# Residuals and a second bias preloaded into PSUM ahead of the products, in a transformer block kernel

## The chip, the cores and the metric

The kernel runs on one core of one Trainium2 chip. The metric is device time in microseconds of one execution. Three executions of the kernel before gave 504.6 us (median), 504.41 us and 506.51 us. The engines of the core are TensorE (PE in the profile; its weight loads are PEld), VectorE (DVE), ScalarE (ACT), GpSimd (POOL) and SyncE (SP, which here only issues DMAs). PSUM is the on-chip memory that the matmuls write into; it has eight banks of 128 x 512 fp32.

## What is computed

A pre-norm transformer block on x of 2048 tokens by 512 features, in fp32: sliding-window attention (32 heads of 16, window of 8 with dilation 2), its output product with a residual, and a second part with a squared ReLU. Cut to what matters here:

```python
h  = x + attention(layernorm(x)) @ wo            # the residual x is added to the output product
r  = relu(layernorm(h) @ w1 + b1)                # 512 -> 1792
h2 = h + (r * r) @ w2 + b2                       # 1792 -> 512, the second bias b2
```

## The kernel before

The 2048 tokens are 16 tiles of 128 rows, numbered `t`, in four groups `u = t // 4` of four tiles. Every fp32 product is made of three matmuls of operands split into a high and a low part (`mm3`, line 218): high x high, low x high, high x low. A product of 512 x 512 for one tile is 12 matmuls of 128 x 128 by 128 x 512.

The program is written out by hand in slots: a slot issues the PE work of a stretch, and then the chores that are due on the other engines. `at(d, f)` puts a chore among those at the end of the slot that is `d` ahead, `after(d, f)` behind these, and between the two `pump` issues pieces of attention on DVE until the DVE work that has been planned (`now["dve"]`) is as long as the PE work (`now["pe"]`). Every chore on DVE adds its planned time with `dve(...)`, so a chore that leaves DVE lets attention be issued earlier. Each engine carries out its own instructions in the order in which they were issued.

Attention is on DVE, POOL and ACT: DVE multiplies the queries with the keys (L340) and sums (L374), takes the maximum (L391) and subtracts it (`ex<-ex,mx`, L393); ACT takes the exponential (L397); DVE multiplies with the values (L351), POOL adds up (L408) into the output tile `o`. The queries come to PSUM with a copy by ACT (`qp`, L268).

The work has three stretches:

- up to about 165 us, the query, key and value products of all tiles (in four PSUM banks by turns), and between them the output products of tiles 0 to 3;
- from there to about 420 us, for u = 0, 1 and 2, the 14 slots of the second part of group u. A slot has `mlp1` (12 matmuls, L228, into a bank of two that take turns, `mm1` and `mm0`), whose ReLU with bias is taken by ACT (`hidden`, L876, then the square L877 and the high part `rh`, L152), and, three slots later, `mlp2` (12 matmuls, L900, that sum into four banks `acc` over all slots). In the same slots attention goes on for the next group, and the output products of its four tiles (`wo_product`, line 688) are put between, into the same two banks as `mlp1`;
- the last group, u = 3, with products put together in another way (L823).

What belongs to one output product of tile `t`, before the change: ACT puts the attention output `o` into two planes (`turn_split`, L621), a DMA transposes them, ACT joins them (`turn_join`, L630) and takes the high part `oh` (or `ohl` for every fourth tile, t = 2, 6, 10, 14; the name of its pool differs only), DVE the low part `ol`. Then PE runs 12 matmuls `wo`. Then `h_add` (line 664): DVE adds the residual out of SBUF to the PSUM bank (`h<-wo,h`, L666), and `norm_stats` takes mean and variance of the sum on DVE (L163, L164) and has POOL make the scale of them (three small instructions, `rs`). Then ACT normalises (`hn<-h,rs`, L196), POOL adds the second bias b2 to h (`add_b2`, L679), and h is written to DRAM (`spill`) to be read back when group t // 4 is finished. At the end of a group, `finish` (line 904) adds h to each `acc` on DVE (L908) and writes out.

SBUF tiles of 128 x 512 come from one ring of 15 (`row`).

Of the kernel before, what the change touches and what calls it, by code (L numbers as in the profile page):

```python
# [17 lines left out]
KB = D // P  # L18
FB = F // P
R = 4  # L20
# [38 lines left out]
def block_kernel(ctx, tc, x, wqkv, wo, w1, b1, w2, b2, out):  # L59
# [113 lines left out]
                                    scalar2=-1.0, op0=ALU.mult, op1=ALU.mult)  # L173
        (at if soon else after)(0, finish)

    def act_stats(key, src):

        nm = small.tile([P, 2], F32, name="nm", bufs=3)
        sq = small.tile([P, 1], F32, name="sq", bufs=3)
        rs = small.tile([P, 2], F32, name="rs", bufs=4)  # L180
        scrap = row("scrap")
        nc.scalar.activation(scrap, src, AF.Identity, accum_out=nm[:, 0:1])
        nc.scalar.activation(nm[:, 1:2], nm[:, 0:1], AF.Identity, scale=-1.0 / D)
        nc.scalar.activation(scrap, src, AF.Square, bias=nm[:, 1:2], accum_out=sq)
        stats[key] = nm, rs

        def finish():
            nc.gpsimd.tensor_scalar(out=rs[:, 1:2], in0=sq, scalar1=1.0 / D, scalar2=EPS,
                                    op0=ALU.mult, op1=ALU.add)
            nc.gpsimd.tensor_tensor(out=rs[:, 0:1], in0=rs[:, 1:2], in1=mhalf, op=ALU.pow)  # L190
            nc.gpsimd.tensor_tensor(out=rs[:, 1:2], in0=nm[:, 1:2], in1=rs[:, 0:1], op=ALU.mult)
        after(0, finish)
# [22 lines left out]
            lo(nc.vector, d, src, h)  # L215
            dve(0.16 + 0.53 / len(h_dst))

    def mm3(ps, lh, ll, rh, rl, mid=None, at_=2 * KB, lows_last=False):


        terms = [[(l, r, k) for k in range(KB)] for l, r in ((lh, rh), (ll, rh), (lh, rl))]
        if lows_last:
            terms[1:] = terms[:0:-1]
        terms = sum(terms, [])
        for n, (l, r, k) in enumerate(terms):
            if mid and n == at_:
                mid()
            nc.tensor.matmul(ps, l(k), r(k), start=(n == 0), stop=(n == 3 * KB - 1))  # L228


    items = [(s, g0, 2) for g0 in range(0, G, 2) for s in range(RI)]
# [39 lines left out]
    def attention():  # L271
# [40 lines left out]
        for n in range(N + 1):  # L312

            new, old = n < N, n > 0
            while new and not ready(n):
                yield None
            ng = ng1 = 0
            if new:
                s, g0, ng = items[n]
                u, b, e, i0 = where(s)  # L320
                HG = ng * GH
                for j in range(2):
                    load_k(n, j)
                if (n, 0) not in qps:
                    next_q(n, 0)
                lf = logits[:, n % 2, :RI * W * HG].rearrange("p (i w h) -> p i w h", i=RI, w=W)
                mx = small.tile([P, RI, HG], F32, name="mx")
            if old:
                s1, g1, ng1 = items[n - 1]
                e1 = ex.pop(n - 1)  # L330
                sm = small.tile([P, RI, ng1 * GH], F32, name="sm")
                if s1 not in o_t:
                    o_t[s1] = att.tile([P, RI, D], F32, name="o", bufs=3)

            def dots(j):
                kwin = window(ks[n, j], s, [1, GC])
                pr = att.tile([P, RI, W, GH, DH], F32, name="pr", bufs=3)
                if j % 2 == 0:
                    qps["now"] = qps.pop((n, j))
                nc.vector.tensor_tensor(  # L340
                    out=pr.rearrange("p i w h d -> p i w (h d)"),
                    in0=qps["now"][:, j % 2].unsqueeze(2).to_broadcast([P, RI, W, GC]),
                    in1=kwin, op=ALU.mult)
                load_k(*ahead(n, j, 2))
                return pr

            def weigh(j):
                load_v(n - 1, j)
                vwin = window(vs[n - 1, j], s1, [DH, GH], [1, DH])
                p2 = att.tile([P, RI, W, GH, DH], F32, name="pr", bufs=3)  # L350
                nc.vector.tensor_tensor(  # L351
                    out=p2, in1=vwin, op=ALU.mult,
                    in0=e1[:, :, :, j * GH:(j + 1) * GH].unsqueeze(4).to_broadcast(
                        [P, RI, W, GH, DH]))
                sums.append((p2, o_t[s1], (g1 + j) * GC, s1))
                load_v(*ahead(n - 1, j, 2))

            for j in range(max(ng, ng1)):
                if j < ng:
                    pr = dots(j)  # L360
                    yield 1.22
                if old and j == 0:
                    nc.vector.tensor_reduce(out=sm, in_=e1.rearrange("p i w h -> p i h w"),
                                            axis=X, op=ALU.add)
                    yield 0.23 + 0.035 * ng1
                if 0 < j < ng1 or 0 < j == ng1 < ng:
                    if j == 1:
                        nc.vector.tensor_tensor(
                            out=e1, in0=e1, op=ALU.mult,
                            in1=sm.unsqueeze(2).to_broadcast([P, RI, W, ng1 * GH]))  # L370
                    weigh(j - 1)
                    yield 1.55 if j == 1 else 1.26
                if j < ng:
                    nc.vector.tensor_reduce(out=lf[:, :, :, j * GH:(j + 1) * GH], in_=pr, axis=X,  # L374
                                            op=ALU.add)
                    yield 1.22
                    if j % 2:
                        next_q(*((n, j + 1) if j + 1 < ng else (n + 1, 0)))
                if old and j == 0:
                    nc.vector.reciprocal(sm, sm)  # L380
                    yield 0.26
            if new and b == 0:
                nc.vector.tensor_tensor(
                    out=lf, in0=lf, op=ALU.add,
                    in1=mask[:, i0:i0 + RI].unsqueeze(3).to_broadcast([P, RI, W, HG]))
                yield 0.16 + 0.07 * ng
            if old and ng1 >= ng:
                weigh(ng1 - 1)
                yield 1.26
            if new:  # L390
                nc.vector.tensor_reduce(out=mx, in_=lf.rearrange("p i w h -> p i h w"), axis=X,  # L391
                                        op=ALU.max)
                nc.vector.tensor_tensor(out=lf, in0=lf, op=ALU.subtract,  # L393
                                        in1=mx.unsqueeze(2).to_broadcast([P, RI, W, HG]))
                ex[n] = lf
                yield 0.42 + 0.15 * ng
                nc.scalar.activation(lf, lf, AF.Exp, scale=DH ** -0.5)  # L397
# [263 lines left out]
        hi_T(tr, hs_)  # L661
        lo_T(tr, hs_, ls_)

    def h_add(t, ps):
        h = hs[t]
        nc.vector.tensor_tensor(out=h, in0=ps, in1=h, op=ALU.add)  # L666
        dve(0.7)
        if t in AS:
            after(0, act_stats, t, h)
        else:  # L670
            norm_stats(t, h, R <= t < 14)

    def h_norm(t):
        hn[t] = row("hn")
# [9 lines left out]
    def unspill(t):  # L684
        hs[t] = row("h")
        nc.sync.dma_start(hs[t], h_d[t])

    def wo_product(t, slots):
        ps = turn["mm"].tile("wo")
        oh, ol = oT.pop(t)  # L690
        mm3(ps, lambda k: oh[:, k, :], lambda k: ol[:, k, :],
            lambda k: wo_h[:, k, :], lambda k: wo_l[:, k, :], lows_last=t in OV)
        for n, (fn, a) in zip(slots, ((h_add, (t, ps)), (h_norm, (t,)), (add_b2, (t,)),
                                      (spill, (t,)))):
            (at if fn is h_add else after)(n + (fn is add_b2), fn, *a)

# [190 lines left out]
    def mlp2(u, f, acc, js, first=False, last=False, mid=None):  # L889
# [7 lines left out]
        for n, (l, w, j) in enumerate(terms):  # L897
            if mid and n == len(terms) // 2:
                mid()
            nc.tensor.matmul(acc[j], l[:, j * P:(j + 1) * P], w[f],  # L900
                             start=(first and n < len(js)),
                             stop=(last and n >= len(terms) - len(js)))

    def finish(t, a):
        u, i = divmod(t, R)
# [106 lines left out]
    def first_phase(t0):  # L1012
        def chores(m):
# [15 lines left out]
                dve(HOLD)  # L1029
            for t in range(R):  # L1030
                if k == OT[t]:
                    at(0, load_h, t)
                    o_T(t)
                if t in HV and k == HK[t][0]:
                    at(0, h_split, t)
                    after(0, turn_dma, ("h", t))
                if t in HV and k == HK[t][1]:
                    at(0, turn_join, ("h", t))
                if k == WO[t]:
                    wo_product(t, (1, 3, 4, 6))  # L1040
                    now["pe"] += 2.73
# [53 lines left out]
    for u in range(R - 1):  # L1095
# [11 lines left out]
        for i in js:  # L1107
            t = R * (u + 1) + i
            if not end:
# [10 lines left out]
                if t in HV:  # L1120
                    h0 = 11 + i
                    turned += [(h0, midway, 0, h_split, t), (h0, after, 0, turn_dma, ("h", t)),
                               (h0 + 2, at, 0, turn_join, ("h", t))]
                for p, *what in ((LH[i] - a, at, 0, load_h, t), *turned,
                                 (WP[i] - a, wo_product, t, (0, 1, 2 + 3 * a + b, 3 + 3 * a + b))):
                    todo.setdefault(p, []).append(what)
                p, h = (HP[i], i % 2) if u < 2 else HL[i]
# [16 lines left out]
        for p in range(FB + LAG):  # L1144
            more = 0.0
            if p == FB:
                run(due)
                dve(HOLD)
            if u < 2 and p == FB - 2:
                dve(HOLD)  # L1150
            for fn, *a in sorted(todo.get(p, []), key=lambda x: x[0] is wo_product):
# [107 lines left out]
```

## Time and profile before

| | us |
|---|---|
| median of three executions | 504.6 |
| the profiled execution, first to last instruction (its span) | 501.7 |
| PE busy | 496.2, 2422 matmuls |
| DVE busy | 382.9 |
| ACT busy | 298.3 |
| POOL busy | 356.2 |
| DVE, adds of the residual (L666), 16 | 10.9 |
| DVE, statistics of h (L163), 16 | 11.1 |
| POOL, adds of b2 (L679), 16 | 21.2 |

An engine is busy from the start to the end of each of its instructions. Matmuls overlap in the pipeline, so the busy time of PE does not say that it ran at its peak: the distance from one matmul's start to the next's says more. A wait is put down to the instruction whose end let the waiting one go. The profiled execution ends 2.9 us before the median time of the three; what lies around the span (start and end of an execution) is in the time and not in the span.

### The profile page before, as it was taken

Reading aid. Unit: us, or ns where it says so; the run is one execution under the profiler, and the core shown is the slowest. Engines: PE = TensorE matmul, PEld = TensorE weight load, DVE = VectorE, ACT = ScalarE, POOL = GpSimd, SP = SyncE. Lnnn points to the kernel's source line nnn. Section 1 sums busy time; section 2 is a strip of 40 time slices with the busy share of each in tenths; the row PEclk is TensorE's granted clock in tenths of the full one; section 3 lists DMA queues with packets and bytes.
Section 4 is the critical chain, followed back from the end, with each engine's and each line's share of the span. In section 5 each row is a group of like instructions: output and inputs, shape, how many; then the busy total and the mean of one; then the engine's idle time right before and its main releaser. Section 6 shows DMA issues by size and latency. Waiting matters only on the chain.

```text
span 501.7 us, 7533 instructions
## 1 busy us (share of the span) xinstructions
PE 496.2 (99%) x2422; PEld 421.2 (84%) x2422; DVE 382.9 (76%) x520; ACT 298.3 (59%) x538; POOL 356.2 (71%) x434
## 2 busy tenths in 40 slices
PE   8999999999999999999999999999999999999997
PEld 7999888888888888888888888888888888998986
DVE  6479899988989989788879998888975147833223
ACT  4635777668346758378564555755555837666551
POOL 5714898886685999969777877769799464775610
PEclk9999999999999999999999999999999999999999
DMA  9668979989698989679577756967665472354112
GB/s 275 202 205 243 300 237 312 270 273 275 212 223 256 299 277 260 205 216 237 190 254 209 215 146 192 237 209 242 210 159 115 112 197 84 137 161 143 64 43 84
DMA packets 109359, 102.61 MB, mean 205 GB/s; under 512 B 29448, under 2 KB 77832, under 8 KB 109320
## 3 DMA queue, kind: packets, MB, share of 16 engines
q1 hardware_dynamic: 108376, 101.61, 69.5%
q10 hardware_dynamic: 944, 0.52, 0.3%
q8 instruction: 19, 0.31, 0.3%
q14 instruction: 20, 0.16, 0.1%
HBM read 72.65 MB, written 24.25 MB: 193 GB/s over the span
## 4 chain that ended last, share of the span: by engine, by line
PE 98%; DMA 1%; ACT 0%; ACTq 0%; DVE 0%; issue 0%
PE mm L228 49%; PE acc L900 30%; PE wo L228 9%; PE mm L823 7%; PE tr L201 2%; DMA wraw<-in_A_wqkv_dram 1%; PE half L923 0%; ACTq L562 0%; ACT big_h L152 0%; ACT xh L152 0%; PE tr L730 0%; DVE h L925 0%
## 5 line engine op out<-in xcount | busy, mean ns | idle before, releaser
L408 POOL TENSOR_TENSOR pr<-pr 128x512 f32<-128x512 f32 (+1 forms) x128 | 133.9, 1046 | 35.1 <-DVE pr L351 29.7
L228 PE MATMUL mm<-big_l,w_h 128*128 128x512 f32 x336 | 88.4, 389 | 0.0
L351 DVE TENSOR_TENSOR pr<-ex,v 128x1024 f32<-128x1024 f32 x64 | 78.0, 1220 | 12.7 <-POOL o L408 9.8
L340 DVE TENSOR_TENSOR pr<-qp,k 128x1024 f32<-128x1024 f32 x64 | 76.8, 1200 | 11.1 <-ACT qp L268 7.6
L374 DVE TENSOR_REDUCE ex<-pr 128x64 f32<-128x1024 f32 x64 | 78.5, 1226 | 2.0
L228 PEld LDWEIGHTS mm<-big_l,w_h 128*128 128x128 f32 x336 | 63.0, 188 | 13.2 <-issue 0.2
L155 POOL TENSOR_TENSOR rl<-r,rh 128x512 fp32r<-128x512 f32 x42 | 55.2, 1317 | 22.3 <-ACT rh L152 22.2
L228 PE MATMUL mm<-big_l,xh 128*128 128x512 f32 (+1 forms) x208 | 55.8, 378 | 0.0
L228 PE MATMUL mm<-big_h,xh 128*128 128x512 f32 (+1 forms) x208 | 53.6, 379 | 0.8 <-ACT xh L152 0.8
L228 PE MATMUL mm<-big_h,xl 128*128 128x512 f32 (+1 forms) x208 | 52.7, 375 | 0.0
L900 PE MATMUL acc<-big_l,rh 128*128 128x512 f32 x190 | 52.2, 390 | 0.0
L900 PE MATMUL acc<-big_h,rh 128*128 128x512 f32 x190 | 52.1, 391 | 0.0
L900 PE MATMUL acc<-big_h,rl 128*128 128x512 f32 x190 | 51.7, 389 | 0.0
L228 PE MATMUL mm<-big_l,w_l 128*128 128x512 f32 x168 | 44.9, 389 | 0.0
L228 PEld LDWEIGHTS mm<-big_h,xh 128*128 128x128 f32 x208 | 37.7, 188 | 7.7 <-ACT xh L152 1.9
L228 PEld LDWEIGHTS mm<-big_h,xl 128*128 128x128 f32 x208 | 38.2, 188 | 6.1 <-DVE xl L155 0.3
L900 PEld LDWEIGHTS acc<-big_h,rl 128*128 128x128 f32 x190 | 35.7, 188 | 7.4
L900 PEld LDWEIGHTS acc<-big_l,rh 128*128 128x128 f32 x190 | 35.5, 188 | 7.4
L228 PEld LDWEIGHTS mm<-big_l,xh 128*128 128x128 f32 x208 | 37.5, 188 | 4.9
L900 PEld LDWEIGHTS acc<-big_h,rh 128*128 128x128 f32 x190 | 34.9, 188 | 6.7
L876 ACT ACTIVATE r<-mm,b_sb 128x512 f32<-128x512 f32 x42 | 28.8, 685 | 18.9 <-PE mm L228 18.1
L228 PEld LDWEIGHTS mm<-big_l,w_l 128*128 128x128 f32 x168 | 31.5, 188 | 6.6
(163 smaller groups left out, 912.3 us busy)
## 6 DMA issues: line engine op xcount, KB each, us to landing
k<-qkv_d SPq DMA_DIRECT2D x48, 288.0 KB, 3.5
v<-qkv_d SPq DMA_DIRECT2D x48, 288.0 KB, 3.9
qkv_d<-y SPq DMA_DIRECT2D x18, 512.0 KB, 4.1
big_l<-w2l_d SPq DMA_DIRECT2D x24, 256.0 KB, 2.6
xt<-in_A_x_dram SPq DMA_DIRECT2D x16, 256.0 KB, 4.1
q<-qkv_d SPq DMA_DIRECT2D x32, 128.0 KB, 3.1
h<-in_A_x_dram SPq DMA_DIRECT2D x16, 256.0 KB, 3.8
h_d<-h SPq DMA_DIRECT2D x16, 256.0 KB, 2.5
```

The source lines that it names most:

```text
L155: eng.tensor_tensor(out=dst, in0=src, in1=h, op=ALU.subtract)
L201: nc.tensor.transpose(tr[:, k, :], src[:, k * P:(k + 1) * P], ident)
L228: nc.tensor.matmul(ps, l(k), r(k), start=(n == 0), stop=(n == 3 * KB - 1))
L340: nc.vector.tensor_tensor(out=pr.rearrange("p i w h d -> p i w (h d)"), in0=qps["now"][:, j % 2].unsqueeze(2).to_broadcast([P, RI, W, GC]) ...
L351: nc.vector.tensor_tensor(out=p2, in1=vwin, op=ALU.mult, in0=e1[:, :, :, j * GH:(j + 1) * GH].unsqueeze(4).to_broadcast([P, RI, W, GH, DH]))
L374: nc.vector.tensor_reduce(out=lf[:, :, :, j * GH:(j + 1) * GH], in_=pr, axis=X, op=ALU.add)
L408: nc.gpsimd.tensor_tensor(out=dst, in0=p2[:, :, :w], in1=p2[:, :, w:2 * w], op=ALU.add)
L823: nc.tensor.matmul(ps, sta[y][:, k], mov[x][:, k], start=(first and q == 0), stop=(last and q == len(terms) - 1), skip_group_check=True)
L876: nc.scalar.activation(r, ps, AF.Relu, bias=b1_sb[:, f:f + 1])
L900: nc.tensor.matmul(acc[j], l[:, j * P:(j + 1) * P], w[f], start=(first and n < len(js)), stop=(last and n >= len(terms) - len(js)))
```

## The change

**The output product.** A new chore `wo_seed(t)` takes the PSUM bank of the product one slot ahead of it (two half slots in the first stretch), and ACT copies the residual into it. The product's first matmul then has no start flag, so that all 12 add to what is in the bank. Behind the product, `h_stats` takes the place of `h_add`: ACT reads the bank, writes the sum to h in SBUF and its sum over the row to `nm` in the same instruction (L182 of the changed kernel), scales that to the mean (L184), and takes the sum of squares with a second pass (L185); POOL makes the scale of it with three small instructions, as before. DVE has no part in it any more.

**The second bias.** For tiles 4 to 11 (groups 1 and 2) `add_b2` on POOL is left out. For u = 1 and 2 ACT copies b2 into the four `acc` banks at the end of the third slot of the group (`bias`), and the first `mlp2` adds to it. Tiles 0 to 3 and 12 to 15 keep `add_b2`.

**Two moves.** In the first stretch the load of the residual is issued three half slots earlier (three ahead of `OT[t]`). In attention, where the next item is not smaller than the one before (`ng1 <= ng`), the sum of the exponentials (`sm<-ex`, L363 before) is issued behind the first sum of products instead of ahead of it.

```diff
-    def act_stats(key, src):
+    def act_stats(key, src, dst=None):
...
-        nc.scalar.activation(scrap, src, AF.Identity, accum_out=nm[:, 0:1])
+        nc.scalar.activation(scrap if dst is None else dst, src, AF.Identity, accum_out=nm[:, 0:1])
+        src = src if dst is None else dst
         nc.scalar.activation(nm[:, 1:2], nm[:, 0:1], AF.Identity, scale=-1.0 / D)
         nc.scalar.activation(scrap, src, AF.Square, bias=nm[:, 1:2], accum_out=sq)
...
-            nc.tensor.matmul(ps, l(k), r(k), start=(n == 0), stop=(n == 3 * KB - 1))
+            nc.tensor.matmul(ps, l(k), r(k), start=(n == 0 and not seed),
+                             stop=(n == 3 * KB - 1), skip_group_check=seed)
...
-                if old and j == 0:
+                if old and j == 0 and ng1 > ng:
                     nc.vector.tensor_reduce(out=sm, in_=e1.rearrange("p i w h -> p i h w"),
...
                 if old and j == 0:
+                    if ng1 <= ng:
+                        nc.vector.tensor_reduce(out=sm, in_=e1.rearrange("p i w h -> p i h w"),
+                                                axis=X, op=ALU.add)
+                        yield 0.23 + 0.035 * ng1
                     nc.vector.reciprocal(sm, sm)
...
-    def h_add(t, ps):
-        h = hs[t]
-        nc.vector.tensor_tensor(out=h, in0=ps, in1=h, op=ALU.add)
-        dve(0.7)
...
-            norm_stats(t, h, R <= t < 14)
+    def h_stats(t, ps):
+        act_stats(t, ps, hs[t])
...
+    def wo_seed(t):
+        seeded[t] = turn["mm"].tile("wo")
+        nc.scalar.copy(seeded[t], hs[t])
...
-        ps = turn["mm"].tile("wo")
+        ps = seeded.pop(t)
...
+            if fn is not add_b2 or t // R in (0, R - 1):
+                (at if fn is h_stats else after)(n + (fn is add_b2), fn, *a)
...
-                             start=(first and n < len(js)),
+                             start=(first and u in (0, R - 1) and n < len(js)),
...
+    def bias(acc):
+        for a in acc:
+            nc.scalar.copy(a, b2_sb)
...
-                    at(0, load_h, t)
...
+                if k == OT[t] - 3:
+                    at(0, load_h, t)
+                if k == WO[t] - 2:
+                    at(0, wo_seed, t)
...
+                                 (WP[i] - a - 1, at, 0, at, 0, wo_seed, t),
...
+            if u and p == LAG - 1:
+                at(0, bias, acc)
```

On PE every matmul stands where it stood; only the start flags differ. Three places on ACT show what moves.

**Place 1**: ACT in group u = 0, up to the high part `ohl` of tile 6. `pl<-o` at L621 and L630 (L628 and L637 of the changed kernel) are the split and the join of the attention output, `r` and `rh` the ReLU, square and high part of a `mlp1`. Before:

```order
L621 COPY pl<-hn 128x1024
L268 COPY qp<-q 128x256
L196 ACTIVATE hn<-h,rs 128x512
L152 CAST big_h<-raw_2516 128x512
L876 ACTIVATE r<-mm,b_sb 128x512
L877 ACTIVATE r<-r 128x512
L152 CAST rh<-r 128x512
L630 COPY pl<-o 128x1024
L152 CAST ohl<-pl 128x512
L621 COPY pl<-hn 128x1024
```

Now:

```order
L271 COPY qp<-q 128x256
L628 COPY pl<-hn 128x1024
L404 ACTIVATE ex<-ex 128x256
L197 ACTIVATE hn<-h,rs 128x512
L152 CAST big_h<-raw_2558 128x512
L885 ACTIVATE r<-mm,b_sb 128x512
L886 ACTIVATE r<-r 128x512
L152 CAST rh<-r 128x512
L637 COPY pl<-o 128x1024
L152 CAST ohl<-pl 128x512
L694 COPY wo<-h 128x512
L628 COPY pl<-hn 128x1024
```

The copy of the residual (`wo<-h`) now stands between `ohl` and the next split, and an exponential (`ex<-ex`) that stood behind place 2 before now stands ahead of the join.

**Place 2**: ACT between the join of tile 7 and the next `hidden`, a few instructions on. Before:

```order
L630 COPY pl<-o 128x1024
L152 CAST oh<-pl 128x512
L268 COPY qp<-q 128x256
L397 ACTIVATE ex<-ex 128x256
L152 CAST w_x<-raw_2658 128x512
L876 ACTIVATE r<-mm,b_sb 128x512
```

Now:

```order
L637 COPY pl<-o 128x1024
L152 CAST oh<-pl 128x512
L182 ACTIVATE h,nm<-wo 128x512
L184 ACTIVATE nm<-nm 128x1
L185 ACTIVATE scrap,sq<-h,nm 128x512
L694 COPY wo<-h 128x512
L271 COPY qp<-q 128x256
L152 CAST w_x<-raw_2707 128x512
L885 ACTIVATE r<-mm,b_sb 128x512
```

The sum and statistics of tile 6 and the residual of tile 7 stand between tile 7's high part and the next ReLU; the exponential is gone from here.

**Place 3**: ACT at the start of group u = 1, from the last part of the normalised h (`big_l<-tr`) on. Before:

```order
L152 CAST big_l<-tr 128x2x128 x4
L876 ACTIVATE r<-mm,b_sb 128x512
L877 ACTIVATE r<-r 128x512
L152 CAST rh<-r 128x512
L268 COPY qp<-q 128x256
L876 ACTIVATE r<-mm,b_sb 128x512
L877 ACTIVATE r<-r 128x512
L152 CAST rh<-r 128x512
```

Now:

```order
L152 CAST big_l<-tr 128x2x128 x4
L404 ACTIVATE ex<-ex 128x256
L885 ACTIVATE r<-mm,b_sb 128x512
L886 ACTIVATE r<-r 128x512
L152 CAST rh<-r 128x512
L885 ACTIVATE r<-mm,b_sb 128x512
L886 ACTIVATE r<-r 128x512
L152 CAST rh<-r 128x512
L916 COPY acc<-b_sb 128x512 x4
L885 ACTIVATE r<-mm,b_sb 128x512
```

Four copies of b2 stand behind the second `hidden` of the group, and an exponential ahead of the first.

More of the change, by code (lines that the diff above doesn't have):

```diff
@@ L216, in lo_T, with mm3 @@
             dve(0.16 + 0.53 / len(h_dst))
-    def mm3(ps, lh, ll, rh, rl, mid=None, at_=2 * KB, lows_last=False):
+    def mm3(ps, lh, ll, rh, rl, mid=None, at_=2 * KB, lows_last=False,
+            seed=False):
         terms = [[(l, r, k) for k in range(KB)] for l, r in ((lh, rh), (ll, rh), (lh, rl))]
@@ L662, in h_parts @@
         lo_T(tr, hs_, ls_)
-    def h_add(t, ps):
-        h = hs[t]
-        nc.vector.tensor_tensor(out=h, in0=ps, in1=h, op=ALU.add)
-        dve(0.7)
-        if t in AS:
-            after(0, act_stats, t, h)
-        else:
-            norm_stats(t, h, R <= t < 14)
+    def h_stats(t, ps):
+        act_stats(t, ps, hs[t])
     def h_norm(t):
@@ L686, in unspill @@
         nc.sync.dma_start(hs[t], h_d[t])
+    seeded = {}
+    def wo_seed(t):
+        seeded[t] = turn["mm"].tile("wo")
+        nc.scalar.copy(seeded[t], hs[t])
     def wo_product(t, slots):
-        ps = turn["mm"].tile("wo")
+        ps = seeded.pop(t)
         oh, ol = oT.pop(t)
         mm3(ps, lambda k: oh[:, k, :], lambda k: ol[:, k, :],
-            lambda k: wo_h[:, k, :], lambda k: wo_l[:, k, :], lows_last=t in OV)
-        for n, (fn, a) in zip(slots, ((h_add, (t, ps)), (h_norm, (t,)), (add_b2, (t,)),
+            lambda k: wo_h[:, k, :], lambda k: wo_l[:, k, :], lows_last=t in OV, seed=True)
+        for n, (fn, a) in zip(slots, ((h_stats, (t, ps)), (h_norm, (t,)), (add_b2, (t,)),
                                       (spill, (t,)))):
-            (at if fn is h_add else after)(n + (fn is add_b2), fn, *a)
+            if fn is not add_b2 or t // R in (0, R - 1):
+                (at if fn is h_stats else after)(n + (fn is add_b2), fn, *a)
     hh, hl = [[big_l[:, n:n + 2].rearrange("p k (i c) -> p k i c", i=R) for n in ns]
@@ L900, in mlp2 @@
             nc.tensor.matmul(acc[j], l[:, j * P:(j + 1) * P], w[f],
-                             start=(first and n < len(js)),
-                             stop=(last and n >= len(terms) - len(js)))
+                             start=(first and u in (0, R - 1) and n < len(js)),
+                             stop=(last and n >= len(terms) - len(js)),
+                             skip_group_check=u in (1, 2))
+    def bias(acc):
+        for a in acc:
+            nc.scalar.copy(a, b2_sb)
     def finish(t, a):
```

## The prediction

> **What bounds the kernel now.** I read the page first: span, busy time and the chain that ended last.
>
> ```profile
> span 501.7 us, 7533 instructions
> PE 496.2 (99%) x2422; PEld 421.2 (84%) x2422; DVE 382.9 (76%) x520; ACT 298.3 (59%) x538; POOL 356.2 (71%) x434
> PE 98%; DMA 1%; ACT 0%; ACTq 0%; DVE 0%; issue 0%
> ```
>
> PE is busy almost from end to end, and 98% of the chain is PE following itself. Then I asked the table of waits for PE alone (who, for whom, us in total, times, longest), and the chain in order of time (start, length, what) for how fast PE goes:
>
> ```profile
> PE tr L952 <- POOL ident masks.py:199: 1.3, 1, 1.3
> PE mm L228 <- ACT xh L152: 0.8, 1, 0.8
> ...
> 228.46 2.95 PE wo L228 x12
> 231.41 2.72 PE mm L228 x12
> 234.13 2.72 PE acc L900 x12
> 236.85 2.72 PE wo L228 x12
> ```
>
> PE waits 2.1 us in the whole execution, 1.3 of them at its first instruction, which the change doesn't touch. A group of 12 matmuls takes 2.72 us, the same whether it is `mm`, `acc` or `wo`: 227 ns from start to start. One `wo` group, that of tile 6, took 2.95, so 0.23 more. So work that is taken from DVE and POOL can shorten the time only by what PE loses to it: at most 0.8 + 0.2 = 1.0 us, about 0.2%. I count below 0.5% (2.5 us) as no change, since that is about what a measurement of this kernel can tell; faster by that much is nearly shut out. The question is what new waits PE gets.
>
> **What is removed.** The 16 residual adds and 16 statistics on DVE, and 8 of the 16 adds on POOL (groups of instructions: count | busy, mean ns | idle before, for whom):
>
> ```profile
> L666 DVE TENSOR_TENSOR h<-wo,h 128x512 f32<-128x512 f32 x16 | 10.9, 682 | 19.3 <-PE wo L228 19.2
> L163 DVE BATCH_NORM_STATS2 st<-h 128x6 f32<-128x512 f32 x16 | 11.1, 695 | 0.5
> L164 DVE BATCH_NORM_AGGREGATE mv<-st 128x2 f32<-128x6 f32 x18 | 3.3, 182 | 0.6
> L679 POOL TENSOR_TENSOR h<-h,b_sb 128x512 f32<-128x512 f32 x16 | 21.2, 1336 | 0.0
> ```
>
> DVE loses 16 x (682 + 695 + 182) ns = 24.9 us, and 19.2 us in which it stood and waited for a product; POOL loses 8 x 1336 ns = 10.7 us. Neither is on the chain, so this is worth 0 by itself. It does move attention forward.
>
> **What is added.** All of it is on ACT. The rows of the nearest operations:
>
> ```profile
> L268 ACT COPY qp<-q 128x256 f32<-128x256 f32 x32 | 12.0, 375 | 25.3 <-DMA q<-qkv_d 16.0 <-DVE pr L340 8.4 <-DVE ex L368 0.9
> L152 ACT CAST rh<-r 128x512 fp32r<-128x512 f32 x56 | 34.8, 622 | 2.3
> L876 ACT ACTIVATE r<-mm,b_sb 128x512 f32<-128x512 f32 x42 | 28.8, 685 | 18.9 <-PE mm L228 18.1 <-POOL pr L408 0.8
> L184 ACT ACTIVATE scrap<-xt,nm 128x512 f32<-128x512 f32 x10 | 7.3, 726 | 0.3
> L183 ACT ACTIVATE nm<-nm 128x1 f32<-128x1 f32 x10 | 2.0, 203 | 0.3
> L182 ACT ACTIVATION_READ_ACCUMULATOR scrap<-xt 128x1 f32 x10 | 1.9, 193 | 0.0
> ```
>
> A copy of 128 x 512 from SBUF to PSUM isn't in the trace. It lies between the copy of half the width to PSUM (375 ns) and the cast of the full width to SBUF (622); I take 600, by the full width. The sum out of PSUM I put at the 685 of L876, the read of its accumulator at 193, the mean at 203, the second pass at 726: 1.8 us. ACT gets 16 x (0.6 + 1.8) + 8 x 0.6 = 43 us more, 298 to 341 us, 68% of the span. That isn't a bound, but ACT works in order, and PE now waits for two things that it did not wait for: a product for its residual copy, and the next user of that bank for ACT's sum instead of DVE's. So I look for places where ACT comes close to PE. The POOL part (three small instructions for the scale) stays.
>
> **Place 1 and 2** (ACT, then PE, in order of time: start, length):
>
> ```profile
> 226.51 1.17 ACT L630 COPY pl<-o 128x1024 uint16<-128x1024 uint16 x1
> 227.71 0.62 ACT L152 CAST ohl<-pl 128x512 fp32r<-128x512 f32 x1
> ...
> 234.19 0.62 ACT L152 CAST oh<-pl 128x512 fp32r<-128x512 f32 x1
> 234.71 0.37 ACT L268 COPY qp<-q 128x256 f32<-128x256 f32 x1
> 236.90 0.37 ACT L397 ACTIVATE ex<-ex 128x256 f32<-128x256 f32 x1 [1.82 <-DVE ex L393]
> ...
> 228.39 1.20 PE L228 MATMUL wo<-wo_h,ohl 128*128 128x512 f32 x4
> 236.69 1.07 PE L228 MATMUL wo<-wo_h,oh 128*128 128x512 f32 x4
> ```
>
> `ohl` of tile 6 is ready at 228.33 and PE starts at 228.39: no slack. With the copy behind it (0.5 more, as ACT's instructions overlap by some 0.1) PE would start at 228.9. At place 2, `oh` is ready at 234.81, then 1.8 and 0.6 give 237.2, with the 0.5 of place 1 237.7, where PE wants 236.69: 1.0 us late in both places together. Behind the copy stand a ReLU and its high part, and `mlp1` waits for that; it moves by as much as PE does.
>
> **The same in u = 1** (tile 10): there the order puts the copy behind a whole `hidden`.
>
> ```profile
> 316.38 0.62 ACT L152 CAST rh<-r 128x512 fp32r<-128x512 f32 x1
> ...
> 316.51 1.07 PE L228 MATMUL wo<-wo_h,ohl 128*128 128x512 f32 x4
> ```
>
> 317.00 + 0.55 = 317.55 against 316.51: 1.0 us late. In sum 2.1 us if ACT gets to these places no earlier than now. But it gets there earlier:
>
> ```profile
> 214.62 0.37 ACT L397 ACTIVATE ex<-ex 128x256 f32<-128x256 f32 x1 [4.99 <-DVE ex L393]
> 217.80 1.05 ACT L621 COPY pl<-o 128x1024 uint16<-128x1024 uint16 x1 [2.08 <-POOL o L408]
> ...
> 307.50 1.05 ACT L621 COPY pl<-o 128x1024 uint16<-128x1024 uint16 x1 [2.13 <-POOL o L408]
> ```
>
> The run of ACT that leads to place 1 starts at 217.80, when attention's output is ready, and ACT stood 4.99 + 2.08 us before; the run to tile 10 starts the same way at 307.50. By 217 us six tiles' adds and statistics are gone from DVE, 6 x 1.56 = 9.4 us, so the output is there, and what ACT has to fit in is one sum (1.8 us, from the end of tile 5's product, near 212) and a copy. I put the start some 2 us earlier than 217.80, and the 0.5 + 0.5 us are covered. By 307 it is ten tiles, 15.6 us. I therefore take 0.2 us for the three places, near the covered end, and keep 2.1 for the range. Tiles 4, 5, 8 and 12 have more room as they are.
>
> **Place 3**, the bias (ACT, then PE):
>
> ```profile
> 255.54 0.62 ACT L152 CAST rh<-r 128x512 fp32r<-128x512 f32 x1
> 256.92 0.69 ACT L876 ACTIVATE r<-mm,b_sb 128x512 f32<-128x512 f32 x1 [0.76 <-POOL pr L408]
> ...
> 259.39 1.07 PE L900 MATMUL acc<-big_h,rh 128*128 128x512 f32 x4
> ```
>
> The copies start at 256.16 and take 4 x 0.5 + 0.1 to 4 x 0.6, until 258.6 at the latest; PE wants the first `acc` at 259.39. Hidden by the lead of three slots, with 0.8 us left; without it 2.4 us twice, 4.8. They must wait for `finish` on DVE; its four adds (0.68 each) end at 252.8 now and may move by two attention steps of 1.2. The ReLU behind moves from 256.92 to 258.6, and `mlp1` needs its bank two groups behind 256.9, at 262.3.
>
> **The moves.** Loading the residual earlier puts 0.4 us of SP in front of some loads of keys and weights, four times; attention pays, and it has gained. In the slots of u = 0 to 2 the load stays where it is, two slots or more (2 x 2 x 2.72 = 10.9 us) ahead of the copy. The move of `sm` costs nothing in instructions. The extra `scrap` tile shortens the ring of 15: a writer could wait for an older reader, by the order at places as near as before; 0.
>
> [...] The trace, in two stretches (us; then busy time of PE, PEld, DVE) and a group of the second:
>
> ```profile
> 165.00:250.00 85.00, 85.00 (x379) 70.13 (x379) 76.00 (x94) 55.31 (x92) 75.60 (x81) 1.00 0.84 242
> 338.00:420.00 82.00, 82.00 (x366) 67.84 (x365) 50.45 (x64) 49.90 (x75) 63.66 (x73) 1.00 0.61 165
> ...
> 350.29 2.72 PE mm L228 x12
> ```
>
> DVE is busy 76.0 / 85 = 89% in the one and 50.5 / 82 = 62% in the other, and a group takes 2.72 us in both. [...]
>
> **The rivals.**
>
> *ScalarE holds PE back by an exponential that comes too early* (slower). By the order the exponentials are issued about one item earlier, ahead of the join of tile 6 and in front of ReLUs at tiles 5, 8 and 11. An `ex` that DVE hasn't finished blocks all of ACT:
>
> ```profile
> ACT ex L397 <- DVE ex L393: 36.8, 15, 6.5
> ```
>
> The mean wait is 36.8 / 15 = 2.45 us, the longest 6.5. Ahead of tile 6 nothing absorbs it: +2.45; at tile 8 `mlp1` leaves some 2.2 us, so +0.25; with the 2.1 us of the copies 4.8 us: 509.4. With 6.5 at tile 6 alone it is 513. It decides at the point where DVE's subtraction ends later than ACT arrives. For it: ACT is blocked that way now, 15 times. Against it: DVE gains 1.56 us a tile and no longer stops for the product.
>
> *ACT isn't earlier, but no exponential blocks*: +2.1, 506.7, within 0.5%.
>
> [...] *The change doesn't do what it says*, the room on DVE isn't used: DVE waits elsewhere, the time is that of the forecast.
>
> **How the numbers follow.** The sum against the profiled execution: 501.7 + 0.2 = 501.9; 2.9 us lie between that span and the median, so 504.8 us. Chances: the forecast (0 to 1.5 us of new waits) 0.64, ACT not earlier 0.17, an exponential that blocks 0.15, shorter groups 0.02, a gain of up to 1 us 0.02. Range: 503.9 (the 1.0 us of PE's waits gained, rounded) to 507.3 (2.1 us, and 0.6 for the spread of the runs, whose highest was 506.5); what is left out is most of the blocking exponential. Faster by over 0.5%: 0.02; within: 0.83; slower: 0.15.
>
> **What would show it.** Right: PE's waits stay below 2 us from 120 us on; the `wo` groups take 2.72; DVE has more idle time in the stretch from 165 to 420 us, and ACT's waits for `ex` and `o` are shorter; `acc` starts at once at the first `mlp2` of u = 1 and 2. Wrong: PE waits for `wo<-h` (the copy) or `acc<-b_sb` by name, ACT's wait for `ex` grows above 37 us, or a wait for the ReLU's bank appears at L228. An instruction that gets longer on PE, in rows that are not waits, would overthrow the bound itself.

## The result, and the profile after

The changed kernel takes 522.3 us (median of 4 runs, 520.8 to 523.7), the kernel before 504.5 us beside it (503.8 to 506.5): ratio 1.034, 95% interval 1.032 to 1.037. It is slower by 17.8 us; 504.8 us were predicted, in a range up to 507.3.

The page of the changed kernel: span, busy time, the chain that ended last.

```profile
span 521.9 us, 7577 instructions
PE 503.4 (96%) x2422; PEld 424.1 (81%) x2422; DVE 360.9 (69%) x472; ACT 334.8 (64%) x642; POOL 343.3 (66%) x426
PE 26%; ACT 4%; DVE 4%; POOL 3%; issue 2%; DMA 2%; DVEq 0%; POOLq 0%; ACTq 0%
```

DVE and POOL lost about what the prediction took from them (22.0 us of busy time where it had 24.9, and 12.9 where it had 10.7), ACT got 36.5 us more. But PE, 99% busy before, is 96% busy in a longer span, and the chain no longer is PE alone. PE's waits say for whom (us in total, times, longest):

```profile
PE wo L230 <- DVE ol L155: 6.0, 3, 2.7
PE mm L230 <- DVE big_l L155: 2.3, 2, 1.4
PE mm L230 <- ACT xh L152: 1.4, 1, 1.4
PE wo L230 <- ACT wo L694: 1.4, 1, 1.4
...
PE mm L230 <- DVE xl L155: 1.1, 1, 1.1
PE tr L739 <- ACT hn L197: 0.6, 1, 0.6
```

The largest wait is for VectorE, from which work was taken: for `ol`, the low part of attention's output, which the last four matmuls of a `wo` product read. The seed (L694), at which the prediction looked, has 1.4 us in one wait.

How `ol` of tile 5 came late: ACT, then DVE, in order of time (start, length, and in brackets the idle time before and what ended it).

```profile
211.05 0.62 ACT L152 CAST oh<-pl 128x512 fp32r<-128x512 f32 x1
211.58 0.59 ACT L182 ACTIVATE h<-wo 128x512 f32<-128x512 f32 x1
...
212.53 0.73 ACT L185 ACTIVATE scrap<-h,nm 128x512 f32<-128x512 f32 x1
...
213.25 0.58 ACT L694 COPY wo<-h 128x512 f32<-128x512 f32 x1
213.76 0.34 ACT L404 ACTIVATE ex<-ex 128x256 f32<-128x256 f32 x1
```

```profile
208.73 0.43 DVE L400 TENSOR_TENSOR ex<-ex,mx 128x256 f32<-128x256 f32 x1
209.07 1.21 DVE L343 TENSOR_TENSOR pr<-qp,k 128x1024 f32<-128x1024 f32 x1
214.14 1.23 DVE L377 TENSOR_REDUCE ex<-pr 128x64 f32<-128x1024 f32 x1 [3.85 <-ACT ex L404]
...
217.71 1.22 DVE L354 TENSOR_TENSOR pr<-ex,v 128x1024 f32<-128x1024 f32 x1
218.86 0.68 DVE L155 TENSOR_TENSOR ol<-pl,oh 128x512 fp32r<-128x512 f32 x1
```

`ol` needs only `oh`, which ACT had at 211.67. It starts at 218.86. Ahead of it in DVE's order stand six steps of attention; the first waits 3.85 us for an exponential, whose logits DVE had given at 209.16, and which stands in ACT's order behind the new sum, squares and seed. PE then starts the third part of tile 5's product at 219.59, after 2.68 us of waiting. Tile 7 is the same with `qp`, where DVE stands for 5.62 us.

In this kernel attention did not get faster for it. All 64 products of `pr<-ex,v` (nanoseconds min/median/max, first and last start in us), before and after:

```profile
L351 DVE TENSOR_TENSOR pr<-ex,v x64: 1190/1224/1226, 39.3 to 378.8; 128x1024 f32<-128x1024 f32 x64
```

```profile
L354 DVE TENSOR_TENSOR pr<-ex,v x64: 1209/1224/1227, 42.3 to 377.9; 128x1024 f32<-128x1024 f32 x64
```

The last one starts at 378.8 and at 377.9 us. It stands earlier in the program and comes at about the same time; PE was held back. The same stretch of both (us; busy time and instructions of PE, PEld, DVE, ACT, POOL; then the granted clock, the busy share of the DMA engines and what they moved in GB/s):

```profile
160.00:260.00 100.00, 100.00 (x445) 82.54 (x445) 89.20 (x109) 65.02 (x108) 84.46 (x90) 1.00 0.83 244
```

```profile
160.00:260.00 100.00, 91.76 (x387) 73.48 (x386) 80.74 (x93) 66.79 (x122) 79.21 (x87) 0.97 0.80 230
```

PE did 387 matmuls instead of 445. From the starts of all matmuls, after less before, 10.6 us are lost between 200 and 262 us, 2.4 between 160 and 180, 2.2 between 340 and 360, 1.8 between 420 and 450, 1.2 at 65 us, and 2.0 in the first 20 us. That last part lies ahead of any changed instruction; from 5 to 10 us the mean granted clock was 0.77 here and 1.00 in the kernel before. Of the 10.6, about 3.1 are matmuls at half clock behind two of the waits: 13 took 427 ns from start to start instead of 227, and a few beside them something between. The last section shows them.

### The profile page after: what moved, and what is told of

It is laid out like the page before. It is cut to its first block, busy times and chain, and to the rows that moved or that the text cites. A ratio compares the mean times of both kernels' runs of the same rounds, so it can differ in the third digit from the quotient of the medians.

```text
span 521.9 us, 7577 instructions
## 1 busy us (share of the span) xinstructions
PE 503.4 (96%) x2422; PEld 424.1 (81%) x2422; DVE 360.9 (69%) x472; ACT 334.8 (64%) x642; POOL 343.3 (66%) x426
## 5 line engine op out<-in xcount | busy, mean ns | idle before, releaser
L230 PE MATMUL mm<-big_l,w_h 128*128 128x512 f32 x336 | 89.7, 393 | 2.5 <-DVE big_l L155 2.3
```

The costliest lines, as they stand in the source:

```text
L230: nc.tensor.matmul(ps, l(k), r(k), start=(n == 0 and not seed), stop=(n == 3 * KB - 1), skip_group_check=seed)
```

## The experiments

**The theories.** A: the credit that the planner kept for VectorE's add and statistics (0.7 + 0.93 us a tile) fell away with them, so attention is issued further ahead; its steps now stand ahead of what PE needs. In the texts below, A1 says that the place of `ol` is all of it, A2 that the order costs by itself, wherever it shows, A3 that it costs only together with ScalarE's new work. B: ScalarE's added load holds PE back by itself. C: the moved reduction `sm`. D: the bias in PSUM. The runs, in us, with the ratio to the kernel before on the same chip:

| kernel | median | ratio (95% interval) |
|---|---|---|
| bias in PSUM alone | 504.5 | 0.9998 (0.9983 to 1.0013) |
| move of `sm` alone | 505.7 | 1.0012 (0.9994 to 1.0030) |
| changed, `sm` back | 518.6 | 1.0273 (1.0245 to 1.0301) |
| changed, `ol` first | 522.3 | 1.0333 (1.0291 to 1.0374) |
| changed, credit 0.8 | 510.6 | 1.0120 (1.0105 to 1.0135) |
| changed, credit 1.63 | 507.1 | 1.0052 (1.0037 to 1.0067) |
| credit 1.63, `sm` back | 507.1 | 1.0037 (1.0020 to 1.0054) |
| credit 1.63, `sm` back, last four tiles on DVE | 504.5 | 1.0006 (0.9994 to 1.0018) |
| credit 1.63, `sm` back, scrap tile of its own | 504.7 | 1.0006 (0.9991 to 1.0020) |
| changed, no squares | 517.4 | 1.0239 (1.0213 to 1.0265) |
| changed, no squares, no seed | 515.0 | 1.0210 (1.0193 to 1.0227) |
| before, no add and statistics, no credit | 511.7 | 1.0128 (1.0089 to 1.0167) |
| before, no add and statistics, credit 1.63 | 504.4 | 0.9995 (0.9974 to 1.0016) |

**Two parts alone.** The bias part of the diff put into the kernel before, and the `sm` part.

> The kernel before with the last part of the change alone: the second bias of tiles 4 to 11 goes into PSUM by ScalarE, and its addition on GpSimd is left away for them. Before runs 504.5 us, the changed kernel 522.3 us. Theory A (the loss comes from attention steps of VectorE that were issued ahead of `ol` and wait for ScalarE): this part has next to nothing of it, 503 to 506 us. Theory B (ScalarE's added copies, sums and squares themselves hold TensorE back): the part has 8 of the copies that ScalarE got, 504 to 508 us. Theory C (the moved reduction `sm` waits for the exponential): 503 to 505 us. Theory D (the bias in PSUM, or the second layer's matmuls without a first clear, is what costs): 510 us or more.

> The kernel before with the move of the reduction `sm` alone (behind the reduction of `pr` that shares the logits' bank, instead of ahead of it). Theory A (attention ahead of `ol`): 503.5 to 506 us, as the steps keep their places against `ol`. Theory B (load of ScalarE): 504 to 505 us. Theory C (the move itself costs, and the added wait of 1.2 us at 64 us of the changed kernel's trace is its first sign): 508 us or more, with TensorE waiting for `xl` and `ol` in the trace.

Neither can be told from the kernel before. D falls, and C as a cause by itself.

**The credit.**

```diff
     def h_stats(t, ps):
         act_stats(t, ps, hs[t])
+        dve(1.63)
```

> The changed kernel, with 1.63 us of planned time on VectorE kept for each tile's removed addition and statistics, so that attention is issued no further ahead than in the kernel before; no instruction is added or left out. Theory A (attention ahead of `ol`): most of the 17.8 us comes back, 505 to 511 us, and the waits of TensorE for `ol` (6.0 us in 3) fall under 2 us. Theory B (load of ScalarE): nothing comes back, 519 to 524 us. Theory C (the moved `sm`): nothing comes back, 519 to 524 us.

No instruction differs, only the order, and 15.2 of the 17.8 us come back; PE's waits for `ol` are gone. B can have the remaining 2.5 us at most by itself.

**`sm` back in its place** (the changed kernel without that part of the diff).

> The changed kernel with the reduction `sm` put back where it was. Theory A (attention ahead of `ol`): the reduction only stands beside the steps that wait, 518 to 524 us. Theory B (load of ScalarE): 520 to 524 us. Theory C (the moved `sm` waits behind the exponential and holds VectorE): most comes back, 505 to 512 us.

518.6: 3.8 us come back, at the low end of A's range and far less than C. With the credit the move is worth nothing (507.1 with it and without, below), so it costs only in the dense order. How, is not shown by itself: in the order above, `sm` is one of the six steps ahead of `ol`, but PE's waits for `ol` only fall from 6.0 to 5.4 us; a wait of 1.1 us for `xl` is gone, and of the two stretches at half clock behind waits for `ol` one is left (0.53 from 216.20 to 219.60 us; 1.00 from 249.20 to 252.00, behind the other).

**`ol` ahead of attention.**

```diff
-        (at if n or t >= 12 else midway)(n, lo_T, tr, [oT[t][0]], [oT[t][1]])
+        at(n, lo_T, tr, [oT[t][0]], [oT[t][1]])
```

> The changed kernel with one order changed: the subtraction that writes `ol` (and `ohl`) is issued ahead of the attention steps of its slot for all tiles, so that no attention step that came forward stands between `oh` and `ol`; attention itself stays as far ahead as in the changed kernel (522.3 us). Theory A1 (it is `ol` behind attention steps which wait for ScalarE): the waits for `ol` (6.0 us in the changed kernel) and the reduced clock behind two of them (some 3.6 us) go, and 509 to 515 us are left, as the waits for the seed and for `big_l` stay. Theory A2 (attention that is too far ahead is late as a whole and only shows up at `ol` first): the wait moves to the next item that VectorE owes, 517 to 523 us.

Nothing comes back. My first form of the theory (A1), that `ol`'s place is the fault, fell. In the trace the waits for `ol` are gone and a longer one has come at tile 6, for an item of ACT and not, as A2 had it, of DVE (ACT, then PE):

```profile
230.12 0.37 ACT L404 ACTIVATE ex<-ex 128x256 f32<-128x256 f32 x1 [2.27 <-DVE ex L400]
...
234.84 0.62 ACT L152 CAST ohl<-pl 128x512 fp32r<-128x512 f32 x1
235.37 0.58 ACT L694 COPY wo<-h 128x512 f32<-128x512 f32 x1
```

```profile
236.00 1.22 PE L230 MATMUL wo<-wo_h,ohl 128*128 128x512 f32 x2 [4.64 <-ACT wo L694]
```

ACT stands 2.27 us for logits from DVE, with `ohl` and the seed behind the exponential in its order. Attention crosses from ACT to DVE and back, both work in order, and what PE needs can stand behind it on either.

**Half the credit** (`dve(0.8)` in place of `dve(1.63)`).

> The changed kernel with 0.8 us of planned time on VectorE kept for each tile, half of what gave 507.1 us; none gives 522.3 us. Theory A2 or A3 (the loss grows with how far attention is issued ahead): 511 to 517 us. If the loss came from one or two places where the order happens to fall badly, and not from the density: 507 to 509 us or 520 to 524 us, by whether these places are hit.

510.6, just below the range given for a loss that grows with the distance: 0, 0.8 and 1.63 us give 522.3, 510.6 and 507.1.

**Less work on ScalarE, the changed order.** One kernel leaves out L184 and the squares, the other also the copy into PSUM.

```diff
-        nc.scalar.activation(nm[:, 1:2], nm[:, 0:1], AF.Identity, scale=-1.0 / D)
-        nc.scalar.activation(scrap, src, AF.Square, bias=nm[:, 1:2], accum_out=sq)
...
+            nc.gpsimd.memset(nm[:, 1:2], 0.0)
+            nc.gpsimd.memset(sq, 512.0)
...
-        nc.scalar.copy(seeded[t], hs[t])
```

> The changed kernel without ScalarE's scaling of the sum and its pass of squares for the output product's statistics (about 0.8 us for each of 16 tiles; two constants take their place, so the norm behind them is not the reference's); order, seeds and sums stay. If the attention steps ahead of `ol` wait for ScalarE behind that new work (theory A with ScalarE's queue as the second half of it): each wait for `ol` becomes shorter by about as much, and the reduced clock behind them goes: 513 to 519 us. If the order alone makes the wait and ScalarE's new work has no part in it: 521 to 524 us. If ScalarE's new work is all of it (theory B): under 509 us.

> The changed kernel's order with about half of ScalarE's new work left out: the residual is not copied into PSUM (so it is missing from the sum), and the scaling of the sum and the pass of squares are replaced by constants; the pass that takes the product out of PSUM stays. Attention is issued as far ahead as in the changed kernel (522.3 us; without the squares alone it took 517.4 us). Theory A2 in the form `attention in denser order is too much for VectorE by itself`: 514 to 518 us. Theory A3 (attention in denser order and ScalarE's new work are both needed, as each attention step crosses from ScalarE to VectorE and back and both engines work in order): 505 to 511 us.

4.9 and another 2.5 us come back. ScalarE's work has its part, but some 10.5 us of loss stay with 14.0 of its 36.5 us of added busy time, in the range of A2. That speaks for a cost of the order by itself, but the pass out of PSUM and the bias copies are still there.

**The order alone.** In the kernel before, the add and the statistics are left out on all engines. One kernel plans nothing for them, so attention stands as in the changed kernel; the other plans 1.63 us, so it stands as before.

```diff
-        nc.vector.tensor_tensor(out=h, in0=ps, in1=h, op=ALU.add)
-        dve(0.7)
...
+        nc.gpsimd.memset(mv, 1.0)
+        stats[t] = mv, rs
+        dve(0.0)
```

> The kernel before with the output product's addition and statistics left out on every engine (the norm takes the residual alone and two constants), and no planned time of VectorE for them: attention then stands in VectorE's order where it stands in the changed kernel, while ScalarE keeps the old, smaller work and has no seed, no sum and no squares. Theory A2 (the order alone: attention steps of VectorE that come forward keep their own pace, and TensorE waits for what stands behind them): 509 to 514 us. Theory A3 (the order hurts only with ScalarE's new work): 504 to 506 us.

> The same kernel with the output product's addition and statistics left out on every engine, and the planned 1.63 us of VectorE kept for each tile, so that attention stands where it stands in the kernel before. It differs from its pair in the order of VectorE's and ScalarE's instructions alone. Theories A2 and A3: 503.5 to 505 us, as nothing is issued further ahead and nothing is added. If leaving the work out has an effect of its own on TensorE: other than that, by its size.

511.7 against 504.4: 7.3 us for the order (A2), with nothing added to any engine but a small fill on POOL, in both kernels. `sm` stands in its old place in both. The trace of the slower one shows it at tile 6 (ACT, then PE):

```profile
227.88 0.37 ACT L397 ACTIVATE ex<-ex 128x256 f32<-128x256 f32 x1 [2.73 <-DVE ex L393]
...
232.47 0.62 ACT L152 CAST ohl<-pl 128x512 fp32r<-128x512 f32 x1
```

```profile
233.14 1.20 PE L228 MATMUL wo<-wo_h,ohl 128*128 128x512 f32 x4 [1.86 <-ACT ohl L152]
```

The exponential that now stands ahead of the join blocks ACT for 2.73 us, and PE waits 1.86. PE's other new waits in this trace are 2.2 us for `big_l` and 1.0 us for `ol`, both from DVE. Attention does come earlier here: its last product with the values starts at 366.2 us instead of 379.1. PE has no use for that and loses all the same. The other kernel of the pair also answers a question of the prediction: with all of the add and the statistics gone and the order kept, the time is that of before.

**The last 2.5 us.** First the credit with `sm` back, then that kernel with tiles 12 to 15 as before.

> The changed kernel with both: the planned 1.63 us of VectorE for each tile kept (that alone gave 507.1 us), and the reduction `sm` put back where it was (that alone gave 518.6 us). If the 2.5 us that are left above the kernel before come from the moved `sm`: 504.3 to 505.5 us. If they come from ScalarE's sums, squares and seeds (theory B, as a small remainder): 506.3 to 507.5 us.

> The changed kernel with the planned 1.63 us kept and `sm` where it was (507.1 us), and the last four tiles (12 to 15) added and measured by VectorE as in the kernel before, without a seed. In the trace of the former, TensorE's largest wait is 1.5 us for tile 15's `hn`, which came at 421.6 us: ScalarE's seed and squares of tile 14 put `rh` 1.2 us later, GpSimd's `rs` of tile 15 came 3.2 us later. If that is the rest: 504.5 to 505.6 us. If ScalarE's new work costs in the other tiles, or the wait has another cause: 506.3 to 507.5 us.

`sm` has no part in it; with the last four tiles back on VectorE none of it can be seen any more. My reading of why had two candidates left. In the trace of the 507.1 us kernel, PE's largest wait, and POOL ahead of it:

```profile
PE tr L736 <- ACT hn L197: 1.5, 1, 1.5
```

```profile
410.45 1.29 POOL L155 TENSOR_TENSOR rl<-r,rh 128x512 fp32r<-128x512 f32 x1 [4.63 <-DMA h_d<-h]
...
416.39 0.19 POOL L189 TENSOR_SCALAR rs<-sq 128x1 f32<-128x1 f32 x1
```

`rl` takes a row of the ring of 15 that `h` shares, and waits until a store of an `h` has read it. Each pass of squares writes its unused output into a row of that ring. So its output went to a tile of its own:

```diff
-        scrap = row("scrap")
+        scrap = (row("scrap") if dst is None else
+                 work.tile([P, D], mybir.dt.uint8, name="scrap", tag="scrap", bufs=1))
```

> The changed kernel with the planned 1.63 us kept and `sm` where it was (507.1 us), and the unused output of the pass of squares no longer takes one of the 15 rows of the ring that `h`, `r`, `rl` and the others share: it goes to a tile of its own (of uint8, for room). ScalarE's sums, squares and seeds all stay. In the trace of the 507.1 us kernel GpSimd's `rl` waits 4.6 us until 410.45 us for the store of an `h` to DRAM, a wait that the kernel before doesn't have, and the late `hn` of the last tile lies behind it. If the ring is the rest: 504.3 to 505.8 us, and that wait is gone. If ScalarE's own work in the last tiles is the rest (its `rh` comes 1.2 us later there): 506.3 to 507.5 us.

504.7 us, with ScalarE's sums, squares and seeds all there. The row that stands for it now:

```profile
409.24 1.47 POOL L155 TENSOR_TENSOR rl<-r,rh 128x512 fp32r<-128x512 f32 x1 [2.25 <-ACT rh L152]
```

`rl` waits for its `rh` and for no store, and PE's wait for `hn` is gone. The ring is worth about 2 us: 2.3 by the medians, 1.6 by the ratios to the kernel before. So the change with the credit kept, `sm` back and the scrap tile moved can't be told from the kernel before; none of the kernels is faster by more than the noise.

## Why the prediction was wrong

- **PE as the bound: right.** What was lost was lost as waits of PE and the clock behind them. Freeing the other engines gained nothing: 504.4 us with DVE's add and statistics gone and the order kept, 504.5 with POOL's eight adds gone.
- **The prices: right or high.** A seed took 584 ns (600 predicted), a sum 596 + 194 (685 + 193), the mean 203, the squares 724 + 187 (726, without their accumulator's read). These add up to 44.5 us (43 predicted); ACT got 36.5 us more of busy time, as neighbours on ACT overlap by some 0.1 us.
- **Place 3 and the move of `sm`: right where they stand alone.** Bias 0.9998, `sm` 1.0012, each within its interval of 1. In the changed order `sm` was worth 3.8 us, which "costs nothing in instructions" didn't see.
- **The step that failed: "It does move attention forward", taken as cover.** From "six tiles' adds and statistics are gone" I concluded "so the output is there", and from that that `ohl` and the seed are in time. The first half is right: in the kernel with the order alone, the split of tile 6, which the prediction put some 2 us ahead of 217.80, starts at 214.95. The second half is not: the planner fills the freed 1.56 us a tile with attention steps, these stand ahead of the join on ACT and ahead of `ol` on DVE, and they wait for each other across the two engines. `ohl` ended at 233.09 there instead of 228.33. In the changed kernel that split starts only at 224.45, behind a sum that stood 5.16 us for tile 5's product. Price: 7.3 us for the order alone, 15.2 with ScalarE's new work and the moved `sm` in the same queues, where the prediction had 0.2 in all.
- **Places 1 and 2 were looked at from ACT to PE only.** At tile 6 the seed was late by 1.4 us, where the prediction had 0.5 without cover. The larger waits, at tiles 5 and 7, were for `ol`, an item of DVE, which the prediction did not follow; tile 5 it had set aside ("have more room as they are").
- **The rival that went the right way** was "an exponential that comes too early", at 0.15 and 509.4 us. The kernel with the order alone shows it at tile 6. It got a small chance by "DVE gains 1.56 us a tile", the same wrong step, and it was priced at single places, while the order was denser at each tile. In the changed kernel itself the longest waits go the other way round: DVE stands for an `ex` (3.9 us) and for `qp` (18.0 us in total, 7.6 before) that are late in ACT's order.
- **Two of the signs did not separate the cases.** DVE had more idle time and ACT's waits for `ex` were shorter (33.5 us, 36.8 before), both listed under "right", in a kernel that lost 17.8 us. The wait for `wo<-h` by name, listed under "wrong", came.
- **The extra scrap tile, put at 0,** cost about 2 us: the ring made POOL wait up to 4.6 us for a store.
- **The clock behind a wait** was not in the sum: 3.1 us in the profiled execution.
- **Shorter groups, at 0.02:** no run shows them. With add and statistics left out and the order kept, PE did 446 matmuls from 160 to 260 us with DVE busy 82%; the kernel before did 445 with DVE busy 89%.
- **One slip in the sums** changes nothing: the forecast with 1.0 us of waits gained gives 503.6 and not 503.9.

What stays open: how the 8 us between the order alone (7.3) and the changed kernel without the credit (15.2) divide. The moved `sm` has 3.8 of them. The other 4 come with the rest of the change, ScalarE's new work above all, but its parts do not simply add up: without the squares 4.9 us came back and without the seeds 2.5 more, and the pass out of PSUM was not taken away by itself in that order.

## What to carry to other kernels

Where a planner sets an order by planned engine time, an instruction that is taken from an engine takes its planned time with it, and the order changes in places that the diff doesn't name: compare the order with that time kept before you judge the edit (15.2 of 17.8 us came back here). Freed time on an engine that works in order is slack only if nothing is issued into it (7.3 us lost here by the order alone). Work that crosses between two such engines stopped both of them here while one part waited for the other (ACT 2.73 us for DVE's logits in the kernel with the order alone, DVE 3.85 us for ACT's exponential in the changed one), and what the bound engine needed waited behind it, in the former although attention got done earlier (its last product with the values at 366.2 us instead of 379.1). An unused output still takes a buffer of its ring, and the one who pays can be another engine (POOL here, 4.63 us in one wait, and about 2 us of the time).

## What the runs showed of the hardware

Two waits of PE in the changed kernel were followed by matmuls at half speed. Behind the waits of 2.68 and 2.48 us, 13 matmuls took 427 ns from start to start instead of 227, and the record of the granted clock has a stretch of 3.41 us at half behind each: 219.29 to 222.70 and 253.43 to 256.84. The first of them with as long a stretch ahead of it (stretch and its length, busy times and instructions; the number behind POOL's is the granted clock):

```profile
215.88:219.29 3.41, 1.03 (x5) 0.53 (x3) 3.32 (x5) 0.64 (x2) 0.27 (x1) 1.00 0.56 167
219.29:222.70 3.41, 3.11 (x7) 2.48 (x8) 1.39 (x2) 0.89 (x3) 3.09 (x5) 0.50 0.57 180
```

The length of the wait alone doesn't decide it. In the kernel without squares and seed a wait of 1.82 us was followed by a mean clock of 0.57 over 4 us (PE in order of time, then the stretch with the wait and the one behind it):

```profile
234.20 1.39 PE L234 MATMUL wo<-wo_h,ohl 128*128 128x512 f32 x4 [1.82 <-ACT ohl L152]
```

```profile
230.00:234.50 4.50, 2.68 (x12) 1.94 (x11) 3.38 (x5) 4.40 (x7) 4.26 (x6) 1.00 1.06 283
234.50:238.50 4.00, 4.00 (x12) 3.09 (x11) 3.17 (x4) 3.50 (x6) 3.14 (x5) 0.57 1.03 308
```

In the changed kernel with `sm` back one of 2.45 us was followed by a clock of 1.00:

```profile
248.94 1.19 PE L230 MATMUL wo<-wo_h,ol 128*128 128x512 f32 x4 [2.45 <-DVE ol L155]
```

```profile
246.00:249.20 3.20, 0.75 (x4) 0.32 (x3) 3.17 (x4) 2.09 (x3) 2.05 (x2) 1.00 0.66 187
249.20:252.00 2.80, 2.80 (x13) 2.29 (x13) 2.77 (x4) 1.77 (x6) 2.48 (x6) 1.00 0.42 126
```

What does decide it is left open here. In the changed kernel the two stretches cost about 3.1 us, so some 1.5 us each.
